# Keeping the parts of k for the second group of rows, and the order of the first weight chunk's work

## The chip, the cores and the metric

One core of one Trainium2 chip. The metric is the time of one execution on the device, in microseconds (us), as the median of several runs. Every time below comes from the profile or from the runs of the kernel before.

## What is computed

Attention that keeps the 32 largest scores of a row, then a dense layer pair with a leaky activation, then a layer that sends each row to one of eight experts. Inputs are float32. q, k and v are 4 x 8 x 576 x 64 (batch, heads, rows, head width).

```python
scores = scale * np.matmul(q, k.transpose(0, 1, 3, 2))
kth = np.partition(scores, -top_k, axis=-1)[..., -top_k:-top_k + 1]
scores = np.where(scores >= kth, scores, -1000000000.0)
attn = softmax(scores)
x = np.matmul(attn, v)                      # 2304 rows of 512
h = x @ w_in                                # 512 x 2048
x = (np.maximum(h, 0.0) + alpha * np.minimum(h, 0.0)) @ w_out
# then: rows with x @ w_skip > 0 add gate * relu(x @ w1[e]) @ w2[e], e by argmax(x @ w_gate)
```

## The kernel before

**Units of work.** A batch has 576 rows: four blocks of 128 (units 0 to 3) and a rest of 64. Heads go in pairs, so a batch has four pairs, and unit 4 takes the rest of both heads of a pair together (the mixed unit). A batch is done in two groups of rows, units 0 and 1, then units 2, 3 and 4; within a group all four pairs follow each other. So each pair of a batch comes up twice, once in either group: 32 pair visits, 80 steps of one unit. After a group its rows go through the dense layers (`moe1`, lines 611 and 657), as a list of small pieces that is dealt out over the following steps.

**Order.** Nothing is scheduled by the machine: `main` writes the instructions out step by step. A step has 14 slots, and the table `STEP` says which part of which unit is issued in which slot. Unit kx+2 has its scores made on PE (`scores`, L417, L411), unit kx+1 has its selection rounds on DVE (`round`, L447, L450) after the fold (`fold`, L438), unit kx its exponentials on ACT (L472) and weights on DVE (`weights`, L480), unit kx-1 is transposed on PE (`turn`, L510 to L516) and copied by ACT (`evac`; R is line 528), unit kx-2 is multiplied by v on PE (`values`, L539, L543) and put into x (`out`, L550, L552). Each engine runs its list in order.

**Heads.** Before a pair's first unit comes its head, `heads`: `load` brings q and k (L321, and L323 for the rest rows), `turn(0)` transposes q on PE, `turn_t` the rest rows of q and k, `turn(1)` k. TensorE multiplies in a short float32 format (F32R), so each operand is kept as two parts: `part` (L330, L331) lets ACT write the high part and a float32 copy `raw_` (two buffers), and POOL subtracts (`sub`, L108) to get the low part. The scores are the sum of three products of parts. The k parts of a pair are a tile `kT` of 2 x 640 columns a partition, in two buffers; L353 copies the rest columns to its other end. `qbd` is the mixed unit's q (L358, L361). The head's pieces are spread over the steps of the pair before it: `hq` is shared out so that each step gets an equal number, the first of them in slot 4, the next in slot 5. Both visits of a pair do the whole head, with the q of their own rows and the whole of k.

**Weights of the dense layers.** They come as 32 chunks of 512 KB in a packed format, and `convert` turns each into parts: ACT copies three times (L277, L279, L281), DVE joins bits (`bits`, L285) and then issues the load of the chunk `AHEAD` = 3 further on, POOL splits (`split`, L291 and L108), SP stores the result (`store`, L297, L300). This goes on during batch 0. The raw chunks lie in halves of the three `wr` buffers, which later hold the dense layers' weights.

**POOL and DVE.** `sub` lets POOL's subtraction wait for DVE's last fold instruction issued before it (`gate`), and `between` holds back `g` parts of the dense layers from slot 9 to slot 1 of the next step. A `ra` tile (six buffers) lives from ACT's line 621 to POOL's `g` part; `held` counts those and lets a new piece begin only below six.

Of the kernel before, what the change touches and what calls it, by code (L numbers as in the profile page):

```python
# [34 lines left out]
AHEAD = 3  # L35
# [12 lines left out]
CV = 4  # L48
# [10 lines left out]
def kernel(  # L59
# [176 lines left out]
    raws, converted, pads = {}, set(), {}  # L236
# [30 lines left out]
    def convert(i):  # L267
# [37 lines left out]
        return none * (CV - 1 if i != 1 else 3 * CV) + [bits] + none * (CV - 1) + [split] + none * CV + [store]  # L305


    def heads(b, p, i, us):
# [3 lines left out]
        own = ((full[0], full[-1] + 1), (0, SF))  # L312
        nats = {}

        def load():
            tail = att.tile([128, 2, D], F32, name="nat_t", tag="nat_t", bufs=2)
            for s, src in enumerate((q, k)):
                nat = att.tile([128, SF, 2, D], F32, name="nat", tag="nat", bufs=2)
                r0, r1 = own[s]
                for h in range(2):  # L320
                    (nc.scalar if s and quick[0] else nc.sync).dma_start(nat[:, r0:r1, h, :],  # L321
                                      src[b, 2 * p + h, 0:SB, :].rearrange("(p r) d -> p r d", p=128)[:, r0:r1])
                (nc.scalar if s and quick[0] else nc.sync).dma_start(tail[s * TL:(s + 1) * TL], src[b, 2 * p:2 * p + 2, SB:S, :].rearrange("h t d -> t h d"))  # L323
                nats[s] = nat
            nats[2] = tail
# [8 lines left out]
        def turn(s):  # L334
            if s == 0:

                hd["q"] = att.tile([128, 2, SB], F32R, name="qT", tag="qT", bufs=2)
                hd["k"] = att.tile([128, 2, S + TL], F32R, name="kT", tag="kT", bufs=2)
# [6 lines left out]
            late.append((HL, lambda: part(hd["k"][:, :, TL:TL + SB] if s else hd["q"][:, :, c0:c1], pt)))  # L345

        def turn_t():
# [3 lines left out]
            def copies():  # L351
                part(hd["k"][:, :, 0:TL], pt[:, TL:128])
                nc.gpsimd.tensor_copy(hd["k"][:, :, S:S + TL], hd["k"][:, :, 0:TL].bitcast(F32))  # L353
# [22 lines left out]
        return hd, [lambda: turn(0), turn_t, lambda: turn(1)]  # L376
# [12 lines left out]
    class Unit:  # L389
# [10 lines left out]
        def scores(self):  # L400
# [4 lines left out]
            for j in range(2):  # L405
                for h in range(self.nh):
                    self.ps[h, j] = ptile() if h and j else psS.tile([128, 512], F32, name="ps", tag="ps")
                for i, (a, b_) in enumerate(((0, 0), (1, 0), (0, 1))):
# [5 lines left out]
                    for h in range(2):  # L414
                        gp = slice(h * 64, (h + 1) * 64)
                        c0 = TL * (1 - h) + j * HALF
                        nc.tensor.matmul(self.ps[h, j][:, 0:HALF], lhsT=hd["q"][gp, a, u * 128:(u + 1) * 128],  # L417
# [162 lines left out]
    def moe1(xx, cols, x2t, base):  # L580
# [20 lines left out]
        def up(wi, f, sg, half, first):  # L601
# [16 lines left out]
            ra = moe.tile([128, 320], F32, name="ra", tag="ra", bufs=6)[:, 0:n]  # L618
# [56 lines left out]
        for hf in range(nhf):  # L675
            for f in range(hf * fs, (hf + 1) * fs):
                for sg, (c0, c1) in enumerate(cols):
                    for half in range(2):
                        one = f % 2 == 0 and sg == 0 and half == 0
                        if half == 0:  # L680
                            parts.append((lambda: room() and held[0] < 6, None))
# [423 lines left out]
    def main(work, exact, hooks=(lambda: [], lambda: [])):  # L1105
# [113 lines left out]
        if not exact:  # L1219
# [3 lines left out]
            for i in range(AHEAD):  # L1223
# [15 lines left out]
        hq.clear()  # L1239
        if exact:  # L1240
# [243 lines left out]
```

## Time and profile before

| | |
|---|---|
| median of 3 runs | 1085.13 us (1083.98 to 1085.79) |
| profiled execution, its own time | 1084.56 us |
| its span in the profile | 1082.8 us |
| busy: PE, DVE, ACT, POOL | 935.1, 922.2, 703.0, 429.7 us |
| mean granted clock of TensorE | 0.947 |
| DMA | 254.13 MB, 235 GB/s in the mean |

Batch 0 runs from the start to about 215 us, the others take some 196 us each, attention ends at about 815 us, the last group's dense layers at about 905 us, and the experts follow.

How to read the rows: times are us from the span's start. A row of a timeline gives start, duration, engine, line, operation, out<-in, shapes and count, and in brackets the engine's idle time before it and what ended it. Merged instructions of a pipelined engine can overlap, so their count times one duration is more than what they take. A row of busy times gives the stretch, its length, the busy us of PE, PEld (weight loads), DVE, ACT and POOL with their instructions, TensorE's granted clock as a share of 2.4 GHz, the DMA engines' busy share and GB/s. A row of the chain gives start, length and what the end of the program waited for then. Engines with a q are their queues.

### The profile page before, as it was taken

What the parts mean: (1) busy time and instruction counts of PE and PEld (TensorE: products, weight loads), DVE (VectorE), ACT (ScalarE), POOL (GpSimd) and SP (SyncE); (2) the same over time, 40 slices, a digit from 0 to 9 for tenths busy, and PEclk for the clock granted to TensorE, in tenths of its full rate; (3) what the DMA queues carried; (4) which work ended last, traced back from release to release, by engine and by line L of the source; (5) the groups of instructions that cost most, each with busy time, mean ns of one, the idle gap of its engine ahead of it and who ended that gap; (6) DMA issues with size and microseconds to landing.
All of it is one profiled execution on the core that took longest, in us unless ns stands there. A gap on an engine that the chain in (4) does not pass through costs nothing.

```text
span 1082.8 us, 21930 instructions
## 1 busy us (share of the span) xinstructions
PE 935.1 (86%) x7270; PEld 844.8 (78%) x7270; DVE 922.2 (85%) x2943; ACT 703.0 (65%) x1804; POOL 429.7 (40%) x577
## 2 busy tenths in 40 slices
PE   4435668998999989989998998999899998798995
PEld 2224458898998878989998898999789897587884
DVE  4999999999999799999989998999895233899972
ACT  6969857765865576567657766866674343597871
POOL 5766754422542334344224433532341330427221
PEclk9966669998999999999999999999999999899998
DMA  7888985665656566766656666665556798899960
GB/s 218 296 276 214 304 259 184 223 214 172 223 190 229 164 214 195 256 222 225 213 167 215 213 252 224 205 225 195 174 203 235 271 349 340 279 356 397 346 234 15
DMA packets 154282, 254.13 MB, mean 235 GB/s; under 512 B 78062, under 2 KB 110830, under 8 KB 137776
## 3 DMA queue, kind: packets, MB, share of 16 engines
q1 hardware_dynamic: 150464, 247.84, 67.6%
q0 software_dynamic: 2496, 4.50, 1.2%
q8 instruction: 59, 0.97, 0.4%
q14 instruction: 63, 0.52, 0.1%
q10 hardware_dynamic: 1200, 0.30, 0.1%
HBM read 224.20 MB, written 29.71 MB: 234 GB/s over the span
## 4 chain that ended last, share of the span: by engine, by line
PE 41%; DVE 37%; issue 6%; ACT 6%; POOL 5%; DMA 5%; SPq 0%; POOLq 0%; DVEq 0%; ACTq 0%
PE pm L657 14%; DVE v L447 8%; PE pm L611 6%; DVE F L438 5%; DVE Ex L480 5%; DVE m L438 4%; DVE F L450 4%; PE px L1033 4%; PE pm L1015 4%; PE px L543 4%; DVE ra L624 3%; PE ps L417 2%; PE pt L510 2%; POOL cv L108 2%; PE pm L723 1%
## 5 line engine op out<-in xcount | busy, mean ns | idle before, releaser
L611 PE MATMUL pm<-x,wr 128*128 128x256 f32 (+1 forms) x1536 | 248.8, 309 | 17.0 <-DVE ra L624 10.3
L657 PE MATMUL pm<-g,wr 128*128 128x256 f32 (+1 forms) x1536 | 236.0, 304 | 4.1 <-DMA wr<-wout 3.5
L611 PEld LDWEIGHTS pm<-x,wr 128*128 128x128 f32 x1536 | 215.7, 194 | 28.2 <-DVE ra L624 14.8
L657 PEld LDWEIGHTS pm<-g,wr 128*128 128x128 f32 x1536 | 210.2, 190 | 9.9 <-issue 4.1
L447 DVE MAX8 v<-F 128x8 f32<-128x72 f32 (+2 forms) x576 | 212.9, 405 | 0.8
L108 POOL TENSOR_TENSOR g<-ra,g 128x256 fp32r<-128x256 f32 (+1 forms) x128 | 104.9, 824 | 185.8 <-ACT g L630 95.6
L480 DVE SCALAR_TENSOR_TENSOR Ex<-sb,v,Ex 128x577 f32<-128x577 f32 x144 | 129.8, 928 | 0.0
L450 DVE MATCH_REPLACE8 F<-v,F 128x72 f32<-128x72 f32 (+1 forms) x432 | 122.8, 289 | 0.0
L422 ACT ACTIVATE sb<-ps 128x288 f32<-128x288 f32 x224 | 80.0, 411 | 62.2 <-PE ps L417 51.3
L630 ACT ACTIVATE g<-ra 128x256 fp32r<-128x256 f32 (+1 forms) x128 | 57.1, 446 | 75.1 <-DVE ra L624 73.3
L472 ACT ACTIVATE Ex<-sb,st 128x576 f32<-128x576 f32 x144 | 104.7, 775 | 0.1
L522 ACT ACTIVATE PT<-pt 128x512 f32<-128x512 f32 x144 | 86.9, 604 | 16.3 <-PE pt L510 15.6
L624 DVE SCALAR_TENSOR_TENSOR ra<-ra,slope,pm 128x256 f32<-128x256 f32 (+1 forms) x128 | 64.6, 505 | 32.1 <-ACT ra L621 30.2
L543 PE MATMUL px<-PT,vt 128*64 128x128 f32 (+1 forms) x1280 | 89.2, 286 | 0.0
L510 PE MATMUL pt<-ident,Ex 128*128 128x128 f32 x576 | 85.9, 281 | 2.6 <-ACT sb L422 2.6
L108 POOL TENSOR_TENSOR x<-xf,x 128x128 fp32r<-128x128 f32 (+1 forms) x80 | 49.3, 617 | 96.0 <-ACT x L552 94.8
L417 PE MATMUL ps<-kT,qT 64*128 64x288 f32 x576 | 79.5, 348 | 6.1 <-ACT kT L330 2.0
L543 PEld LDWEIGHTS px<-PT,vt 128*64 128x64 f32 x1280 | 70.1, 147 | 9.9 <-issue 1.8
L417 PEld LDWEIGHTS ps<-kT,qT 64*128 64x128 f32 x576 | 61.4, 210 | 19.3 <-issue 9.4
L510 PEld LDWEIGHTS pt<-ident,Ex 128*128 128x128 f32 x576 | 70.7, 146 | 3.9 <-ACT sb L422 3.5
L621 ACT ACTIVATE ra<-pm 128x256 f32<-128x256 f32 (+1 forms) x128 | 52.4, 409 | 30.9 <-PE pm L611 28.7
L438 DVE TENSOR_TENSOR F<-m 128x144 f32<-128x144 f32 (+2 forms) x240 | 70.2, 344 | 0.0
(431 smaller groups left out, 1834.8 us busy)
## 6 DMA issues: line engine op xcount, KB each, us to landing
wr<-win SPq DMA_DIRECT2D x64, 1024.0 KB, 4.9
wr<-wout SPq DMA_DIRECT2D x64, 1024.0 KB, 4.9
wraw<-in_moe_w_dram SPq DMA_DIRECT2D x88, 512.0 KB, 6.3
wr<-in_moe_w_in_dram SPq DMA_DIRECT2D x16, 512.0 KB, 6.1
vt<-in_v_dram SPq DMA_DIRECT2D x32, 256.0 KB, 2.8
win<-cv SPq DMA_DIRECT2D x16, 512.0 KB, 4.8
wr<-in_moe_w_out_dram SPq DMA_DIRECT2D x16, 512.0 KB, 5.6
wout<-cv SPq DMA_DIRECT2D x32, 256.0 KB, 4.1
```

What stands on the lines that cost most here:

```text
L108: i = nc.gpsimd.tensor_tensor(o, a, b, op=OP.subtract)
L417: nc.tensor.matmul(self.ps[h, j][:, 0:HALF], lhsT=hd["q"][gp, a, u * 128:(u + 1) * 128], rhs=hd["k"][gp, b_, c0:c0 + HALF], **se)
L438: gate[0] = nc.vector.tensor_tensor(o[:, n_], a[:, n_, 0:w], a[:, n_, w:2 * w], op=op)
L447: nc.vector.max(v8[:, h, r, :], F[:, h, 0:w])
L450: nc.vector.match_replace(out=F[:, h, 0:w], in_to_replace=v8[:, h, r, :], in_values=F[:, h, 0:w], imm_value=NEG)
L472: nc.scalar.activation(self.Ex[:, h, :], self.sb[:, h, :], AF.Exp, bias=self.st[:, 0, h:h + 1], scale=0.125)
L480: nc.vector.scalar_tensor_tensor(self.Exp[:, cs], self.sbp[:, cs], v8[:, h, 3, 7:8], self.Exp[:, cs], op0=OP.is_ge, op1=OP.mult, accum_out ...
L510: nc.tensor.transpose(pt[:, c * 128:(c + 1) * 128], P[:, c0:c0 + 128], ident)
L543: nc.tensor.matmul(x[h * 64:(h + 1) * 64, 0:n], lhsT=hd["vt"][:, h, c, :], rhs=rhs, start=False, stop=(c == SF - 1))
L611: nc.tensor.matmul(hp[:, 0:n], lhsT=w[:, (f % 2) * 8 + a * 4 + d, :], rhs=x[:, d, c0:c1], start=(i == 0), stop=(i == 3 * KD - 1))
L624: nc.vector.scalar_tensor_tensor(ra, ra, slope[:, f:f + 1], hp[:, 0:n], op0=OP.mult, op1=OP.add)
L657: nc.tensor.matmul(op_[:, 0:n], lhsT=w[:, 2 * f + a, :], rhs=g[(hf + ch) * 8 + f, sg][:, gg, 0:n], start=(i == 0), stop=(i == ni - 1))
```

## The change

Each pair's k parts are kept in a place of their own (`kT0` to `kT3`, one buffer each) from a pair's first visit of a batch to its second. The second visit loads no k but the rest rows (which share a transpose with q's), does not transpose k, and makes no k parts. The q tile has room for 256 columns instead of 512, and `ra` five buffers instead of six, with the limit in `moe1` lowered alike. `AHEAD` is 4: three chunks are loaded first, the fourth after the first heads' loads, and from then on `bits` loads four ahead. Chunk 0's `bits` and `split` are issued one slot after its copies.

```diff
-AHEAD = 3
+AHEAD = 4
...
-        return none * (CV - 1 if i != 1 else 3 * CV) + [bits] + none * (CV - 1) + [split] + none * CV + [store]
+        if i == 0:
+            return none + [bits, split] + none * (2 * CV) + [store]
+        return none * (CV - 1 if i > 1 else 3 * CV) + [bits] + none * (CV - 1) + [split] + none * CV + [store]
...
+        fresh = us[0] == 0
...
             for s, src in enumerate((q, k)):
+                if s and not fresh:
+                    nc.sync.dma_start(tail[TL:2 * TL], src[b, 2 * p:2 * p + 2, SB:S, :].rearrange("h t d -> t h d"))
+                    continue
...
-                hd["q"] = att.tile([128, 2, SB], F32R, name="qT", tag="qT", bufs=2)
-                hd["k"] = att.tile([128, 2, S + TL], F32R, name="kT", tag="kT", bufs=2)
+                hd["q"], hd["c0"] = att.tile([128, 2, 256], F32R, name="qT", tag="qT", bufs=2), own[0][0] * 128
+                if fresh:
+                    kept[p] = att.tile([128, 2, S + TL], F32R, name="kT", tag=f"kT{p}", bufs=1)
+                hd["k"] = kept[p]
...
-                part(hd["k"][:, :, 0:TL], pt[:, TL:128])
-                nc.gpsimd.tensor_copy(hd["k"][:, :, S:S + TL], hd["k"][:, :, 0:TL].bitcast(F32))
+                if fresh:
+                    part(hd["k"][:, :, 0:TL], pt[:, TL:128])
+                    nc.gpsimd.tensor_copy(hd["k"][:, :, S:S + TL], hd["k"][:, :, 0:TL].bitcast(F32))
...
-        return hd, [lambda: turn(0), turn_t, lambda: turn(1)]
+        return hd, [lambda: turn(0), turn_t] + ([lambda: turn(1)] if fresh else [])
...
-            ra = moe.tile([128, 320], F32, name="ra", tag="ra", bufs=6)[:, 0:n]
+            ra = moe.tile([128, 320], F32, name="ra", tag="ra", bufs=5)[:, 0:n]
...
-                            parts.append((lambda: room() and held[0] < 6, None))
+                            parts.append((lambda: room() and held[0] < 5, None))
...
-            for i in range(AHEAD):
+            for i in range(AHEAD - 1):
                 conv_load(*convs[i])
...
+        if not exact:
+            conv_load(*convs[AHEAD - 1])
```

The order of SP's queue at the head of the program, before (the `wr` rows are the loads of chunks 3, 4, and 5 and 6; `win` is the store of chunk 0; `nat` are q and k of the third pair, `vt` and `vbd` v of the second):

```order
L369 DMA vt<-in_v_dram 128x2x256
L372 DMA vbd_93<-in_v_dram 64x64 x2
L258 DMA wr<-in_moe_w_in_dram 128x4x256
L297 DMA win_123<-cv 128x1024
L258 DMA wr<-in_moe_w_in_dram 128x4x256
L321 DMA nat<-in_q_dram 128x2x64 x2
L323 DMA nat_t<-in_q_dram 64x2x64
L321 DMA nat<-in_k_dram 128x4x64 x2
L323 DMA nat_t<-in_k_dram 64x2x64
L258 DMA wr<-in_moe_w_in_dram 128x4x256 x2
```

and after the change (the `wr` rows are chunks 3, 4 and 5):

```order
L258 DMA wr<-in_moe_w_in_dram 128x4x256
L379 DMA vt<-in_v_dram 128x2x256
L382 DMA vbd_93<-in_v_dram 64x64 x2
L258 DMA wr<-in_moe_w_in_dram 128x4x256
L297 DMA win_123<-cv 128x1024
L258 DMA wr<-in_moe_w_in_dram 128x4x256
L328 DMA nat<-in_q_dram 128x2x64 x2
L330 DMA nat_t<-in_q_dram 64x2x64
L328 DMA nat<-in_k_dram 128x4x64 x2
L330 DMA nat_t<-in_k_dram 64x2x64
```

The load of chunk 3 moved ahead of the second pair's v, that of chunk 4 ahead of the store of chunk 0, and that of chunk 5 ahead of the third pair's q and k.

The order on ACT in the second group of batch 2, two steps in which the head of the third pair is made (PT and R are the unit's transposes, `ps` the head's), before:

```order
L330 ACTIVATE qT<-ps 128x256
L331 ACTIVATE raw__7629<-ps 128x256
L330 ACTIVATE kT<-ps 128x64
L331 ACTIVATE raw__7640<-ps 128x64
L358 ACTIVATE raw__7645<-ps 128x64
L361 ACTIVATE qbd_95<-ps 64x64 x2
L522 ACTIVATE PT<-pt 128x512
L552 ACTIVATE x<-xf 128x128
L522 ACTIVATE PT<-pt 128x512
L455 ACTIVATE st<-v_7279 128x1
L527 ACTIVATE PT<-px 128x128
L528 ACTIVATE R<-px 128x128
```

and after the change:

```order
L337 ACTIVATE qT<-ps 128x256
L338 ACTIVATE raw__7443<-ps 128x256
L532 ACTIVATE PT<-pt 128x512
L562 ACTIVATE x<-xf 128x128
L532 ACTIVATE PT<-pt 128x512
L465 ACTIVATE st<-v_7100 128x1
L537 ACTIVATE PT<-px 128x128
L538 ACTIVATE R<-px 128x128
```

The copies of k's rest columns and of k are gone; the mixed unit's q (L358 and L361, now L368 and L371) moved to the next step, five rows further on.

The order on PE in the same second step, before and then with the change:

```order
L657 MATMUL pm<-g,wr 128x320 x6
L343 MATMUL ps<-ident,nat 128x128 x4
L510 MATMUL pt<-ident,Ex_143 128x128 x4
L657 MATMUL pm<-g,wr 128x320 x6
L510 MATMUL pt<-ident,Ex_143 128x128 x4
```

```order
L667 MATMUL pm<-g,wr 128x320 x6
L358 MATMUL ps<-ident,nat_t 128x128
L520 MATMUL pt<-ident,Ex_143 128x128 x4
L667 MATMUL pm<-g,wr 128x320 x6
L520 MATMUL pt<-ident,Ex_143 128x128 x4
```

The four transposes of k are gone, and the transpose of the rest rows stands there, which was in the step before.

## Rows read from the trace of the kernel before

**Rows 1.** the page, part 4: the chain of waits by engine

```profile
PE 41%; DVE 37%; issue 6%; ACT 6%; POOL 5%; DMA 5%; SPq 0%; POOLq 0%; DVEq 0%; ACTq 0%
```

**Rows 2.** busy time by stage, second groups of batches 1 and 3

```profile
300.00:413.00 113.00, 103.80 (x905) 95.48 (x900) 103.76 (x382) 71.24 (x215) 42.59 (x65) 0.98 0.60 198
...
697.00:812.00 115.00, 108.24 (x945) 100.36 (x944) 109.78 (x409) 76.73 (x227) 41.61 (x66) 0.99 0.60 201
```

**Rows 3.** the same by stretch, head of the program

```profile
10.00:20.00 10.00, 4.74 (x23) 3.15 (x23) 7.94 (x29) 8.54 (x20) 4.21 (x6) 1.00 0.70 187
20.00:30.00 10.00, 1.33 (x8) 0.98 (x8) 5.86 (x16) 5.38 (x10) 7.24 (x8) 1.00 0.96 283
...
140.00:160.00 20.00, 12.51 (x75) 10.23 (x75) 19.01 (x60) 10.70 (x32) 13.35 (x16) 0.61 0.95 291
```

**Rows 4.** timeline of DVE, head; in brackets the wait before it

```profile
18.23 0.69 DVE L285 SCALAR_TENSOR_TENSOR cv<-cv 128x512 int32<-128x512 int32 x1 [1.31 <-ACT cv L281]
...
24.38 0.91 DVE L285 SCALAR_TENSOR_TENSOR cv<-cv 128x512 int32<-128x512 int32 x1 [2.67 <-ACT cv L281]
...
29.60 1.13 DVE L285 SCALAR_TENSOR_TENSOR cv<-cv 128x512 int32<-128x512 int32 x1 [0.71 <-ACT cv L281]
...
36.24 0.69 DVE L285 SCALAR_TENSOR_TENSOR cv<-cv 128x512 int32<-128x512 int32 x1 [0.90 <-ACT cv L281]
```

**Rows 5.** timeline of ACT, head

```profile
22.38 0.67 ACT L277 ACTIVATE cv<-wr 128x512 f32<-128x512 f32 x1 [1.36 <-DMA wr<-in_moe_w_in_dram]
...
27.60 0.67 ACT L277 ACTIVATE cv<-wr 128x512 f32<-128x512 f32 x1 [3.25 <-DMA wr<-in_moe_w_in_dram]
```

**Rows 6.** timeline of SP's queue, head; last row: of PE

```profile
17.14 0.35 SPq L297 DMA_DIRECT2D win<-cv  x1
...
22.27 1.15 SPq L258 DMA_DIRECT2D wr<-in_moe_w_in_dram  x2
...
31.20 0.69 PE L343 MATMUL ps<-ident,nat 128*128 128x128 f32 x2 [9.33 <-ACT sb L422]
```

**Rows 7.** lines 343 and 330: ns least/median/most, first and last start

```profile
L343 PE MATMUL ps<-ident,nat x192: 270/272/477, 3.9 to 789.7; 128*128 128x128 f32 x192
...
L330 ACT ACTIVATE kT<-ps x64: 203/426/628, 5.7 to 790.0; 128x512 fp32r<-128x512 f32 x32, 128x64 fp32r<-128x64 f32 x32
```

**Rows 8.** timeline of ACT, then PE, third pairs of batches 1 and 2

```profile
347.68 0.22 ACT L358 ACTIVATE raw__4531<-ps 128x64 f32<-128x64 f32 x1 [1.11 <-POOL qT L108]
...
350.04 0.49 PE L539 MATMUL px<-PT,vbd 128*128 128x128 f32 x2 [1.75 <-ACT R L528]
...
550.36 0.49 PE L539 MATMUL px<-PT,vbd 128*128 128x128 f32 x2 [0.99 <-ACT R L528]
```

**Rows 9.** chain of waits in batch 1, then the timeline of DVE

```profile
354.50 0.44 PE ps L343 x4
...
365.05 0.18 DVE L767 TENSOR_REDUCE rc<-lg 128x3 f32<-128x24 f32 x1 [3.80 <-ACT lg L732]
```

**Rows 10.** timeline of DVE, then POOL, in batch 2

```profile
527.79 0.80 DVE L480 SCALAR_TENSOR_TENSOR Ex<-sb,v,Ex 128x577 f32<-128x577 f32 x1
...
528.52 1.84 DVE L480 SCALAR_TENSOR_TENSOR Ex<-sb,v,Ex 128x577 f32<-128x577 f32 x1
...
555.94 1.84 DVE L438 TENSOR_TENSOR F<-sb 128x576 f32<-128x576 f32 x1
...
528.25 1.49 POOL L108 TENSOR_TENSOR kT<-raw__7365,kT 128x512 fp32r<-128x512 f32 x1 [4.62 <-ACT raw__7365 L331]
```

**Rows 11.** timeline of POOL, then DVE, in batch 0

```profile
153.09 0.83 POOL L108 TENSOR_TENSOR kT<-raw__1561,kT 128x64 fp32r<-128x64 f32 x1
153.98 0.70 POOL L353 CAST kT<-kT 128x128 fp32r<-128x128 f32 x1
...
164.01 0.48 DVE L624 SCALAR_TENSOR_TENSOR ra<-ra,slope,pm 128x256 f32<-128x256 f32 x1 [2.73 <-ACT ra L621]
```

**Rows 12.** busy time and granted clock of one stretch

```profile
250.00:270.00 20.00, 16.95 (x129) 15.73 (x128) 18.24 (x84) 11.03 (x30) 5.19 (x9) 0.74 0.48 144
```

More of the change, by code (lines that the diff above doesn't have):

```diff
@@ L235 @@
     wout32 = w_out.bitcast(I32)
-    raws, converted, pads = {}, set(), {}
+    raws, converted, pads, kept = {}, set(), {}, {}
     todo, late, convq, rowq = [], [], [], []
@@ L312, in heads @@
         own = ((full[0], full[-1] + 1), (0, SF))
+        fresh = us[0] == 0
+        assert own[0][1] - own[0][0] <= 2
         nats = {}
@@ L344, in turn @@
                                     ident)
-            late.append((HL, lambda: part(hd["k"][:, :, TL:TL + SB] if s else hd["q"][:, :, c0:c1], pt)))
+            late.append((HL, lambda: part(hd["k"][:, :, TL:TL + SB] if s else hd["q"][:, :, 0:c1 - c0], pt)))
         def turn_t():
@@ L416, in scores @@
                         c0 = TL * (1 - h) + j * HALF
-                        nc.tensor.matmul(self.ps[h, j][:, 0:HALF], lhsT=hd["q"][gp, a, u * 128:(u + 1) * 128],
+                        nc.tensor.matmul(self.ps[h, j][:, 0:HALF], lhsT=hd["q"][gp, a, u * 128 - hd["c0"]:(u + 1) * 128 - hd["c0"]],
                                          rhs=hd["k"][gp, b_, c0:c0 + HALF], **se)
```

## Prediction

> **What bounds the kernel now.** I read the page's chain of waits first: PE has 41% of the time that decides the end and DVE 37% [rows 1], so neither engine is the bound by itself. The busy time by stage says why. In the second group of rows of batch 1 (300 to 413 us) PE is busy 103.80 and DVE 103.76 of 113 us; in that of batch 3 (697 to 812 us) 108.24 and 109.78 of 115 [rows 2]. Both are nearly full, each waits for the other now and then, and work that only one of them loses is lost to the end only where the chain runs over that engine. ACT (71 to 77 us there) and POOL (about 42) have room, but they stand between the two: what they do late, PE or DVE waits for.
>
> The head of the program is another matter. From 10 to 30 us DVE is busy 7.94 and 5.86 of 10 us [rows 3]. Its waits there end with ACT's last copy of a weight chunk (L281), and ACT itself waits 1.36 and 3.25 us for the load of the chunk [rows 4, 5]. Further on in batch 0 DVE has hardly a wait left: from 140 to 160 us it is busy 19.01 of 20 [rows 3].
>
> **The change, part by part.** It does what it says: the order of the built program has no second-group k work, and without the rows of the heads the order on PE, DVE, ACT and POOL is that of before, apart from the first chunk's split on POOL. So the limit of five `ra` tiles moves no instruction; I cost it at nothing, and the cover is that POOL's `g` parts end several us before the tile is wanted again (ACT shows no wait for a `g` part).
>
> *Head.* In the kernel before, the load of chunk 4 stands behind the store of chunk 0, which waits for POOL's split until 17.14 us, and the load of chunk 5 stands behind the q and k loads of the third pair, at 22.27 us [rows 6]. Now the split of chunk 0 stands ahead of the second pair's parts on POOL, the load of chunk 4 goes ahead of the store, and that of chunk 5 ahead of the q and k loads. Both should have landed when ACT asks. Of DVE's three waits (2.67, 0.71 and 0.90, 4.28 together [rows 4]) one piece stays: ACT is free for chunk 4 from 21.02 us (22.38 less its wait), so DVE still waits some 1.3 us for it. Gain **3.0 us**, an estimate. Its ends are 0 and 4.3: zero if the DMA engines, 0.96 busy from 20 to 30 us and 0.95 from 140 to 160 [rows 3], only pass the same bytes in another order. I take a value near the upper end since they are 0.70 busy from 10 to 20 us [rows 3], which is where the loads move to. What the loads are moved past: the store of chunk 0 (nobody reads it for 100 us) and the loads of the third pair, which land later by about two chunk loads; PE takes those only at 31.20 us, after 9.33 us of waiting for something else [rows 6]. The early split puts two POOL instructions under DVE's first fold; that can stretch the fold by about 1.1 us, as below, and DVE's wait of 1.31 us at 18.23 [rows 4] hides it; without that cover the gain would be 1.9.
>
> *PE, 16 pairs.* Each second-group pair loses four transposes of k. One takes 0.27 us in the rows, but they overlap: four have 0.44 us of the chain [rows 7, 9]. 16 x 0.44 = 7.0 us of PE in all, of which only four pairs have them on the chain, one in batch 3, one in batch 2, two in batch 1.
>
> *ACT, 16 pairs.* Two copies of 512 columns and two of 64 go: 0.2 to 0.6 us each [rows 7], some 1.6 us a pair, beside other work. What counts is a wait. A pair's small part (`turn_t`) needs a third buffer `raw_` while there are two, so ACT waits for POOL's q part: 1.11 us at 347.68, and PE behind it 1.75 us for R; in batch 2 PE's wait is 0.99, in batch 3 the same pattern returns [rows 8]. With no k part in between, q and the mixed unit's q have two buffers, and the latter moves to the next step. Those PE waits should go.
>
> *POOL, 16 pairs.* One subtraction of 512 columns, one of 64 and one copy go. Where POOL works on SBUF while DVE runs an instruction with two inputs, both are stretched. DVE's weights instruction takes 0.80 us alone and 1.84 under the k part, its fold 1.84 under the next one, and POOL's part takes 1.49 [rows 10]. Six of the twelve k parts of the later batches fall on such instructions, two in each batch; the rest fall on MAX8 and MATCH_REPLACE, which are not stretched. The Trainium skill, SBUF — State Buffer, section "SBUF: two separate sides", says the shared ports are an exclusive lock, the loser blocking for the other's whole instruction. The rows agree only in the sum: DVE goes on, 1.04 us late, and POOL is late as well. By the rule with POOL's 1.49 a collision would cost 1.49 instead of 1.04, and the two that I count below would give 0.9 us more.
>
> *DMA.* 32 loads of k of 128 KB go from SP's queue; they were asked for a pair ahead of their transposes, and I cost them at nothing, up and down.
>
> *What of it lies on the path.* Batch 0: POOL's small k part and its copy (0.83 and 0.70 us at 153 us) stand ahead of the x part that PE waits for, and DVE waits 2.73 us at 164.01 at the end of that chain [rows 11]. Gain **1.5**, ends 0 and 2.7. Batch 1: here PE leads up to the logits, where DVE waits 3.80 us [rows 9], so PE's 1.75 and 0.44 count: **2.2**. Batches 2 and 3: the first collision (1.04) lies in a stretch that DVE leads, then PE's wait (0.99) and four transposes (0.44) where PE leads: **2.5** each. Against it: the x part, which POOL does behind the k part, now starts earlier and falls on the same DVE instruction; I take off 0.3 us for each of the two collisions counted, **0.6**. What is late next is the x part itself and, in batch 1, DVE.
>
> **Sum**: 3.0 + 1.5 + 2.2 + 2.5 + 2.5 - 0.6 = 11.1 us. The profiled execution took 1084.56 us (span 1082.8), 0.57 below the median of the runs, 1085.13. 1084.56 - 11.1 = 1073.5, and that is the forecast: **1073.5 us**. Lower bound of the gain: only the two DVE collisions less their give-back, 1.5, so 1083.1. Upper bound: 4.3 + 2.7 + 7.2, and the four collisions that I left out at 1.04 each: 18.4, so 1066.2.
>
> **The rivals.** (a) *Hidden*: the DMA engines hold the first 160 us (0.95 busy at its end [rows 3]) and the other engine takes every gap in the later batches. For it: both engines are within 5% to 8% of full [rows 2]. Against it: DVE itself gets shorter by the collisions. Gain 0 to 2: about 1083.5 us. Chance 0.08. (b) *Slower, by TensorE's clock.* PE loses work and waits more for DVE in the second groups. Already from 250 to 270 us, with PE busy 16.95 of 20, the granted clock is 0.74 [rows 12]: 0.26 of the way down, so half of those 20 us ran at 1.2 GHz instead of 2.4, and PE lost 5.2 us of work. If three more such places arise in stretches that PE leads, 15.6 us are lost against 11.1 won: 1089 us; from the third on it decides. Against it: the stretches of batches 1 and 3 are at 0.98 and 0.99 [rows 2] although PE waits there, and the change also takes away PE waits. The Trainium skill, TensorE: Matmul & The Clock Gate, section "Part 1: The HAM clock gate", says that the lower clock is the default and activity lifts it, which speaks against a change that takes work from PE. Chance 0.05. (c) *Gains add up*: DVE gets shorter where it leads and PE where it leads, so that the four other collisions and PE's remaining R waits count, and the later stages of the chain fall into better places: 1064 us. For it: gaps of both kinds stand close together. Chance 0.07.
>
> **How the numbers follow.** The forecast's case has 0.80. Its bounds 1066.2 and 1083.1 together with a third of (c) give the range: **1065.0 to 1082.5**, which leaves out (b), most of (a) and the far side of (c). A measurement of this kernel tells a change from none from about 0.2% (2.2 us) on. Faster: 0.80 + 0.07, and a little of (a): 0.88. Within 0.2%: the rest of (a): 0.07. Slower: 0.05.
>
> **What would show it.** In the profile after: DVE's waits at L285 between 20 and 40 us down to about 1.3 us, ACT's waits for chunk loads there gone, and DVE's eighth chunk (at 36.24 us before) about 3 us earlier; no 1.84 us weights instruction on DVE beside a k part; PE's waits for R in the second groups under 0.5 us; attention ending some 11 us earlier and the tail, from 812 us on, of the same length. The forecast is wrong if the attention's end moves by under 3 us, if the clock in the second groups falls under 0.95, or if the tail grows by what the attention lost.

## The result and the profile after

The changed kernel takes **1066.37 us** in the median (1066.3 to 1066.6, 4 runs) against 1085.46 of the kernel before: ratio 0.9822, 95% interval 0.9803 to 0.9841, so 19.1 us faster. The forecast was 1073.5 in a range from 1065.0 to 1082.5. Sign and range hold; the gain is some 8 us larger than forecast. The profiled execution took 1066.43 us, its span 1064.6.

DVE runs the same instructions in the same order in both kernels. So the start of one DVE instruction in both traces tells how much has been won by then:

| DVE instruction near | before | after | earlier by | forecast up to there |
|---|---|---|---|---|
| the end of the head | 52.8 | 51.0 | 1.75 | 3.0 |
| second group of batch 0, its middle | 152.5 | 149.2 | 3.25 | |
| end of batch 0 | 219.8 | 210.7 | 9.11 | 4.5 |
| start of batch 1's second group | 296.4 | 286.4 | 10.02 | |
| end of batch 1 | 415.0 | 399.4 | 15.60 | 6.7 |
| end of batch 2 | 615.2 | 596.9 | 18.29 | 8.9 |
| end of batch 3 | 811.7 | 791.7 | 20.00 | 11.1 |
| end of the span | 1082.8 | 1064.6 | 18.2 | 11.1 |

The surplus came in two places: from 152 to 220 us, and in the second group of batch 1. Batches 2 and 3 gave 2.7 and 1.7 us where 2.2 each was forecast, and the tail gave 1.8 us back. A share of one batch is uncertain by some 2 us: the changed kernel once more against the run with five `ra` tiles (both below, on two other chips) has 5.9, 6.5, 4.4 and 2.1 us in batches 0 to 3.

The page's chain of waits by engine, which was DVE's nearly as much as PE's [rows 1], is now PE's:

```profile
PE 53%; DVE 28%; ACT 4%; DMA 3%; issue 3%; POOL 2%; SPq 0%; POOLq 0%; ACTq 0%; DVEq 0%
```

Busy time by stage, the same pieces of work as in [rows 2] (columns as there: PE, PEld, DVE, ACT, POOL, then clock, DMA share, GB/s), and the stretch of batch 0 that [rows 3] ends with:

```profile
289.50:397.40 107.90, 100.62 (x891) 92.62 (x886) 101.31 (x381) 66.89 (x201) 33.71 (x55) 1.00 0.60 200
678.50:792.00 113.50, 107.51 (x931) 99.80 (x930) 107.22 (x409) 72.21 (x213) 32.07 (x56) 0.97 0.58 197
...
140.00:160.00 20.00, 16.44 (x132) 14.50 (x132) 19.69 (x62) 12.51 (x38) 10.76 (x14) 0.85 0.90 297
```

The second group of batch 1 lost 3.2 us of PE's busy time, 2.5 of DVE's and 9 of POOL's, and is 5.1 us shorter: more than either engine lost, so waits went too. From 140 to 160 us the granted clock is 0.85 where it was 0.61; the changed kernel on another chip has 0.69 there.

**Head.** Timeline of DVE, line 285 (two chunks of those in [rows 4], then the eighth), the early split's neighbour (line 448, which was 438), and ACT's only wait of 0.4 us or more for a chunk between 20 and 38 us:

```profile
11.47 1.80 DVE L448 TENSOR_TENSOR m<-sb 128x576 f32<-128x576 f32 x1 [0.85 <-ACT sb L432]
...
23.87 1.00 DVE L285 SCALAR_TENSOR_TENSOR cv<-cv 128x512 int32<-128x512 int32 x1 [1.23 <-ACT cv L281]
29.48 1.36 DVE L285 SCALAR_TENSOR_TENSOR cv<-cv 128x512 int32<-128x512 int32 x1
35.16 1.74 DVE L285 SCALAR_TENSOR_TENSOR cv<-cv 128x512 int32<-128x512 int32 x1
...
34.98 0.67 ACT L277 ACTIVATE cv<-wr 128x512 f32<-128x512 f32 x1 [0.40 <-DMA wr<-in_moe_w_in_dram]
```

The waits went as forecast (1.23 left of 2.67, the others gone), but part of them came back as longer instructions beside POOL: the first fold took 0.76 us before and takes 1.80. The eighth chunk is 1.1 us earlier, not 3.

**Batch 0.** Before, ACT stood still behind POOL. Timelines of ACT and PE of the kernel before:

```profile
153.16 0.22 ACT L358 ACTIVATE raw__1566<-ps 128x64 f32<-128x64 f32 x1 [3.19 <-POOL qT L108]
...
154.25 0.30 ACT L552 ACTIVATE x<-xf 128x128 fp32r<-128x128 f32 x1
...
154.60 1.23 PE L611 MATMUL pm<-x,wr 128*128 128x256 f32 x4 [2.09 <-ACT x L552]
```

The same places after (ACT, then POOL, then DVE):

```profile
147.36 0.31 ACT L562 ACTIVATE x<-xf 128x128 fp32r<-128x128 f32 x1 [0.97 <-DVE xf L560]
...
148.62 0.97 POOL L108 TENSOR_TENSOR x<-xf,x 128x128 fp32r<-128x128 f32 x1
...
156.25 0.48 DVE L634 SCALAR_TENSOR_TENSOR ra<-ra,slope,pm 128x256 f32<-128x256 f32 x1
```

ACT no longer waits for POOL, x goes out as soon as DVE has it, and DVE's wait of 2.73 us [rows 11] is down to 0.13. Two shorter waits of DVE for `ra` beside it are gone as well; before:

```profile
158.54 0.48 DVE L624 SCALAR_TENSOR_TENSOR ra<-ra,slope,pm 128x256 f32<-128x256 f32 x1 [0.82 <-ACT ra L621]
...
185.58 0.48 DVE L624 SCALAR_TENSOR_TENSOR ra<-ra,slope,pm 128x256 f32<-128x256 f32 x1 [0.90 <-POOL qbd L108]
```

At these three instructions together DVE's lead over the kernel before grows by 4.5 us.

**Waits for R.** Busy time by line, PE's first multiply of the values (line 539 before, 549 after; x count, then busy us, mean ns, and the idle time before it with what ended it), 140 us to the end of attention, before:

```profile
L539 PE MATMUL px<-PT,vbd 128*128 128x128 f32 (+1 forms) x136 | 27.4, 284 | 8.2 <-ACT R L528 8.2
```

and after:

```profile
L549 PE MATMUL px<-PT,vbd 128*128 128x128 f32 (+1 forms) x137 | 26.6, 276 | 0.2 <-ACT R L538 0.2
```

Nearly all the waits for R are gone, 8.2 us of PE's idle time before; the forecast had counted 3.7 of them (1.75 and twice 0.99).

**Collisions.** DVE in batch 2, the two instructions that took 1.84 us each [rows 10]:

```profile
512.22 0.81 DVE L490 SCALAR_TENSOR_TENSOR Ex<-sb,v,Ex 128x577 f32<-128x577 f32 x1
...
539.49 0.75 DVE L448 TENSOR_TENSOR F<-sb 128x576 f32<-128x576 f32 x1
```

DVE's lead over the kernel before grows by 1.03 us at the first and by 1.10 at the second, which the forecast had left out. In between, DVE loses 0.80 us of it where it then waits longer for PE (2.06 us instead of 1.25).

**Batch 1.** The logits and two `ra` tiles behind them. DVE before, beside the wait of 3.80 us at the logits [rows 9], and then after:

```profile
375.83 0.48 DVE L624 SCALAR_TENSOR_TENSOR ra<-ra,slope,pm 128x256 f32<-128x256 f32 x1 [1.27 <-ACT ra L621]
...
380.99 0.48 DVE L624 SCALAR_TENSOR_TENSOR ra<-ra,slope,pm 128x256 f32<-128x256 f32 x1 [1.16 <-ACT ra L621]
```

```profile
351.41 0.18 DVE L777 TENSOR_REDUCE rc<-lg 128x3 f32<-128x24 f32 x1 [2.52 <-ACT lg L742]
...
361.11 0.48 DVE L634 SCALAR_TENSOR_TENSOR ra<-ra,slope,pm 128x256 f32<-128x256 f32 x1 [0.19 <-issue]
...
365.42 0.47 DVE L634 SCALAR_TENSOR_TENSOR ra<-ra,slope,pm 128x256 f32<-128x256 f32 x1
```

DVE's lead grows by 1.28 us at the logits and by 2.3 at the two `ra` tiles. Two collisions, which the forecast did not count in this batch, give 1.02 and 1.10, of which 0.86 is lost again in a wait for PE.

**Tail.** Timeline of PE, the last block of multiplies, before and then after:

```profile
1066.56 5.72 PE L1033 MATMUL px<-x,hs 128*128 128x512 f32 x24 [2.32 <-DVE orow L1041]
```

```profile
1047.02 7.29 PE L1043 MATMUL px<-x,hs 128*128 128x512 f32 x24 [2.32 <-DVE orow L1051]
```

The same 24 multiplies take 1.57 us longer: nothing in them was changed, they now lie in a stretch of lower granted clock (0.77 from 1047 to 1054.4 us, against 1.00 from 1066 to 1072.5 before). That is most of the 1.8 us given back. In the fourteen traces of this case the block takes 7.15 to 7.33 us nine times and 5.7 five times. The last experiment below, which keeps the whole change, is among the five, so the change does not force the longer block.

### The profile page after: what moved, and what is told of

Same layout as the page of the kernel before. It is cut to its first block, busy times and chain, and to the rows that moved or that the text cites. A ratio compares the mean times of both kernels' runs of the same rounds, so it can differ in the third digit from the quotient of the medians.

```text
span 1064.6 us, 21663 instructions
## 1 busy us (share of the span) xinstructions
PE 925.9 (87%) x7206; PEld 834.4 (78%) x7206; DVE 915.7 (86%) x2943; ACT 684.1 (64%) x1740; POOL 386.0 (36%) x529
## 4 chain that ended last, share of the span: by engine, by line
PE 53%; DVE 28%; ACT 4%; DMA 3%; issue 3%; POOL 2%; SPq 0%; POOLq 0%; ACTq 0%; DVEq 0%
PE pm L667 18%; PE pm L621 10%; DVE v L457 6%; PE px L553 5%; DVE Ex L490 4%; PE px L1043 4%; PE pm L1025 4%; DVE F L448 3%; DVE F L460 3%; PE ps L427 3%; PE pt L520 3%; DVE ra L634 3%; DVE m L448 3%; DMA wr<-wout 2%; PE pm L733 1%
## 5 line engine op out<-in xcount | busy, mean ns | idle before, releaser
L621 PE MATMUL pm<-x,wr 128*128 128x256 f32 (+1 forms) x1536 | 244.8, 307 | 15.4 <-DVE ra L634 10.6
L621 PEld LDWEIGHTS pm<-x,wr 128*128 128x128 f32 x1536 | 212.9, 191 | 27.1 <-DVE ra L634 15.9
L108 POOL TENSOR_TENSOR x<-xf,x 128x128 fp32r<-128x128 f32 (+1 forms) x80 | 46.3, 579 | 112.2 <-ACT x L562 111.2
L448 DVE TENSOR_TENSOR F<-m 128x144 f32<-128x144 f32 (+2 forms) x240 | 66.6, 329 | 0.0
```

Of the source, the lines that this page charges most:

```text
L108: i = nc.gpsimd.tensor_tensor(o, a, b, op=OP.subtract)
L448: gate[0] = nc.vector.tensor_tensor(o[:, n_], a[:, n_, 0:w], a[:, n_, w:2 * w], op=op)
L621: nc.tensor.matmul(hp[:, 0:n], lhsT=w[:, (f % 2) * 8 + a * 4 + d, :], rhs=x[:, d, c0:c1], start=(i == 0), stop=(i == 3 * KD - 1))
```

## The experiments

The twelve runs were made in three sittings of four, each on a chip of its own, on which the kernel before takes a little longer (medians 1090.14, 1089.57 and 1088.39 us). So ratios to the kernel before of the same sitting are compared. The first sitting has the two halves of the change, the smaller `ra` ring and the run without POOL's parts; the second has the changed kernel again, PE's transposes, the old step and the third buffer; the third has the rest. Where a trace of before is needed, the run with five `ra` tiles, from the chip of the first sitting, stands in for it.

**Which half of the change?** The change without its head:

```diff
-AHEAD = 4
+AHEAD = 3
...
-        if i == 0:
-            return none + [bits, split] + none * (2 * CV) + [store]
...
-            for i in range(AHEAD - 1):
+            for i in range(AHEAD):
...
-            conv_load(*convs[AHEAD - 1])
```

> The change without its head: k is kept in four places, but three chunks are loaded ahead as before, chunk 0 is split and stored as before. Theory 1 (the head gives what DVE's first waits show, 1.75 us by 52 us of the span, and all the rest comes from the k work that is gone): 1068 us, 16 to 18 us faster than before, and at the end of batch 0 DVE is 6 to 7 us earlier than before. Rival 2 (the head also carries the gain inside batch 0, where DVE is 9.1 us earlier at 215 us, because its chunks are through sooner): about 1075 us, and DVE at the end of batch 0 at most 3 us earlier than before. Rival 3 (head and k add less alone than together): 1070 to 1073 us.

Measured: 1070.96 us, ratio 0.9818 (0.9803 to 0.9833). The k part alone gives 18 to 21 us. In its trace DVE is 5.2 us earlier than before at 204 us, after being 1.4 late at 52 (6.4 earlier and 0.4 late against the stand-in). Rival 2 falls, and Rival 3 with it: by the ratio, k alone gives rather more than the 16 to 18 us of Theory 1, not less.

The same edit the other way round, on the kernel before, is the head alone:

> The kernel before with the head of the change alone: four chunks ahead, chunk 0's bits and split at once, the fourth load behind the first heads. Theory 1: 1.5 to 2.5 us faster than before, about 1083.3 us, with the k parts' collisions and waits all still there. Rival 2: about 1076 us. My forecast had 3.0 for it, so 1082.4 us. If the early split stretches DVE's first folds and nothing is won by it, 1085.

Measured: 1087.6 us, ratio 0.9974 (0.9963 to 0.9985): 1.6 to 4.0 us. The trace has DVE 2.65 us earlier than before at 52 us and no more than that at 204 us (3.6 and 3.4 against the stand-in, from the same chip). The forecast's 3.0 stands for the head by itself.

The smaller ring of `ra` tiles, on the kernel before:

```diff
-            ra = moe.tile([128, 320], F32, name="ra", tag="ra", bufs=6)[:, 0:n]
+            ra = moe.tile([128, 320], F32, name="ra", tag="ra", bufs=5)[:, 0:n]
...
-                            parts.append((lambda: room() and held[0] < 6, None))
+                            parts.append((lambda: room() and held[0] < 5, None))
```

> The kernel before with five ra tiles in place of six, and the limit that goes with them. All theories that I hold: no change, 1085 us, within 0.2%. If the sixth tile was worth something, slower by 1 us or more, and then the change had to win that back too.

Measured: 1088.59 us, ratio 0.9989 (0.9977 to 1.0001). No cost.

Last, the changed kernel itself, on the chip of the second sitting:

> The changed kernel unaltered, beside the next three on one chip. Expected: ratio to before 0.982, as in the result. Theory 3 (head and k do not add: k alone gave 0.9818): nothing left for the head to add, so 0.980 to 0.983; if they add, 0.9795 or less, since the head alone gave 0.9974.

Measured: 1068.25 us, ratio 0.9805 (0.9789 to 0.9821). Together with 0.9822 of the first chip and 0.9818 for k alone, the head's share within the whole change is between nothing and some 3 us: whether the two parts add stays open.

**Which engine's share of the k work?** The work was put back into the changed kernel step by step. First everything but POOL's:

```diff
-                if s and not fresh:
-                    nc.sync.dma_start(tail[TL:2 * TL], src[b, 2 * p:2 * p + 2, SB:S, :].rearrange("h t d -> t h d"))
-                    continue
...
+        def idle(pt):
+            n = pt.shape[1]
+            raw = att.tile([128, 512], F32, name="raw_", tag="raw_", bufs=2)[:, 0:n]
+            nc.scalar.activation(raw, pt, AF.Copy)
+            nc.scalar.activation(raw, pt, AF.Copy)
...
+            if s and not fresh:
+                late.append((HL, lambda: idle(pt)))
+                return
...
+                else:
+                    idle(pt[:, TL:128])
...
-        return hd, [lambda: turn(0), turn_t] + ([lambda: turn(1)] if fresh else [])
+        return hd, [lambda: turn(0), turn_t, lambda: turn(1)]
```

> The changed kernel with the second groups' k loads, transposes and ACT copies put back (both copies go to the staging tile, nobody reads it), without POOL's subtractions and copy. Against the changed kernel it prices PE's and ACT's part, against the head alone it prices POOL's part. Theory 1a (POOL's parts, by stretching DVE's two-input instructions and by standing ahead of the x part, carry the gain): 1067 to 1070 us. Rival 1b (PE's four transposes and the waits of PE for ACT carry it): 1076 to 1080 us. By my forecast's terms (16 pairs, PE's transposes 0.44 on four of them and waits for R of 1.75 and 0.99, these already gone without POOL's part): 1068.2 us.

Measured: 1080.78 us, ratio 0.9920 (0.9904 to 0.9936); its own runs spread from 1076.1 to 1083.9. Theory 1a falls: with the head and without POOL's parts, 8.7 of the 21 us are left. The rest is not all work of PE and ACT, though. With three pieces in the head again, `turn_t` is back in its old step, which the expectation overlooked, and the runs below price that by itself at 4.8 us.

The same without ACT's copies (loads and PE's transposes stay):

```diff
-                late.append((HL, lambda: idle(pt)))
                 return
...
-                else:
-                    idle(pt[:, TL:128])
```

> The changed kernel with the second groups' k loads and the k transposes on PE put back (four of a pair, nobody reads them), without ACT's copies and without POOL's parts. It splits what the run without POOL's parts (0.992 of before) left between PE and ACT. Theory 4 (ACT's k copies, 1.6 us a pair, stand ahead of the copies of ra, R and the logits that PE and DVE wait for): as the changed kernel within 3 us, 0.982 to 0.985. Rival 5 (the four transposes are what counts, 16 times 0.44 us and more where they sit ahead of the dense layers): 0.988 to 0.991.

Measured: 1077.12 us, ratio 0.9888 (0.9873 to 0.9903). So rival 5's figure came out. But this kernel, too, has `turn_t` back in its old step. Two runs take that apart. The old step alone, with an empty third piece:

```diff
-        return hd, [lambda: turn(0), turn_t] + ([lambda: turn(1)] if fresh else [])
+        return hd, [lambda: turn(0), turn_t] + [(lambda: turn(1)) if fresh else (lambda: None)]
```

> The changed kernel with the second groups' small transposes (turn_t) issued in the step where they stood before, one step earlier than the change has them; nothing else. If the move counts (the mixed unit's q copies sharing a step with the q copies again): slower than the changed kernel by 1 to 3 us, PE's waits for R back. If k's work alone was the load: as the changed kernel within 1 us.

Measured: 1073.18 us, ratio 0.9849 (0.9833 to 0.9864). Without any k work the mere place of one transpose, three small copies and two small subtractions is worth 4.8 us. PE's waits for R came back only in part (1.5 us in its trace, 0.2 in the changed kernel's), and ACT's waits for POOL's q part not at all, so the staging buffer is not the reason.

The old step and the k loads (the `continue` above taken out, no transposes):

> The changed kernel with the second groups' k loads put back and the small transposes in the old step; no transposes, copies or subtractions of k. Between the run with the old step alone (0.985) and the one with loads and PE's transposes (0.989) it tells the DMA's part from PE's. Forecast's step (loads cost nothing): 0.984 to 0.986, as the old step alone. Rival (32 loads of 128 KB crowd SP's queue or the DMA engines): 0.988 or more.

Measured: 1073.53 us, ratio 0.9862 (0.9848 to 0.9876), inside the interval of the run before: the best estimate for the loads is 1.4 us, which is within the error of nothing.

Read downwards, each difference is one share (in thousandths, times 1.089 us; each is uncertain by about 2 us, and the rows come from three chips):

| kernel | ratio | what goes to the next row | us |
|---|---|---|---|
| before | 1 | the head | 2.8 |
| head alone | 0.9974 | POOL's k parts | 5.9 |
| without POOL's parts | 0.9920 | ACT's k copies and their hold on the staging buffers | 3.5 |
| loads and PE's transposes | 0.9888 | PE's k transposes | 2.8 |
| old step and loads | 0.9862 | the k loads | 1.4 |
| old step | 0.9849 | `turn_t` one step later | 4.8 |
| changed kernel | 0.9805 | | 21.2 in all |

**The staging buffer.** The forecast had put the waits for R on the third `raw_` that a head wants. This is the kernel before with one more:

```diff
-            raw = att.tile([128, 512], F32, name="raw_", tag="raw_", bufs=2)[:, 0:pt.shape[1]]
+            raw = att.tile([128, 512], F32, name="raw_", tag="raw_", bufs=3)[:, 0:pt.shape[1]]
...
-                raw = att.tile([128, 512], F32, name="raw_", tag="raw_", bufs=2)[:, 0:TL]
+                raw = att.tile([128, 512], F32, name="raw_", tag="raw_", bufs=3)[:, 0:TL]
```

> The kernel before with three staging buffers raw_ in place of two, and nothing else. My forecast put PE's waits for R (1.75 us in batch 1, 0.99 in batches 2 and 3) on ACT's wait of 1.11 us for the third of these buffers. If that is the mechanism: 2 to 4 us faster, ratio 0.996 to 0.998. Theory 4 (ACT's k copies themselves make R late, the buffer hardly matters): 0.9995 to 1.0005.

Measured: 1081.63 us, ratio 0.9932 (0.9919 to 0.9945): **7.4 us**, about twice what was expected. The mechanism is shown, and its size was wrong: ACT's twelve waits for POOL's q part are gone, and PE's waits for R in the attention come to 3.3 us in its trace against 8.8 in the stand-in's (8.2 on the first chip). Timeline of PE, then DVE, in batch 1 and the busy time of three stretches (the clock is the third column from the end), of the stand-in for before, which is from another chip:

```profile
349.81 0.49 PE L539 MATMUL px<-PT,vbd 128*128 128x128 f32 x2 [1.76 <-ACT R L528]
...
366.33 0.18 DVE L767 TENSOR_REDUCE rc<-lg 128x3 f32<-128x24 f32 x1 [6.57 <-ACT lg L732]
...
348.00:352.00 4.00, 2.24 (x23) 1.74 (x24) 4.00 (x23) 2.40 (x8) 1.82 (x6) 0.86 0.23 94
352.00:356.00 4.00, 4.00 (x28) 3.71 (x27) 3.99 (x9) 1.62 (x5) 0.00 (x0) 0.71 0.00 0
...
372.00:376.00 4.00, 4.00 (x38) 3.61 (x38) 3.67 (x19) 1.92 (x3) 2.87 (x5) 0.65 0.67 195
```

and of the kernel with three buffers:

```profile
347.43 0.49 PE L539 MATMUL px<-PT,vbd 128*128 128x128 f32 x2 [0.49 <-ACT R L528]
...
362.43 0.18 DVE L767 TENSOR_REDUCE rc<-lg 128x3 f32<-128x24 f32 x1 [2.51 <-ACT lg L732]
...
348.00:352.00 4.00, 4.00 (x43) 3.66 (x42) 4.00 (x20) 1.55 (x6) 0.79 (x4) 1.00 0.01 2
352.00:356.00 4.00, 4.00 (x32) 3.99 (x31) 4.00 (x6) 3.64 (x10) 2.27 (x2) 1.00 0.75 250
...
368.00:372.00 4.00, 3.95 (x47) 3.68 (x48) 3.77 (x19) 2.62 (x5) 2.76 (x5) 1.00 0.78 217
```

PE waits 1.76 us for R with PE busy 2.24 of 4 us, and the granted clock falls: 0.86 and 0.71 of full in the two stretches are 0.14 and 0.29 of 4 us of work, at most 1.7 us, lost on top of the wait. DVE's wait for the logits is then 6.57 us; with the third buffer it is 2.51 and the clock stays at 1.00. The wait and the fall together thus cost about 4 us at the logits. This pair alone does not take them apart, since both went. But the kernel before on the first chip has the same wait and keeps its clock there (last section), and its DVE waits 3.80 us at the logits [rows 9]. By that, some 1.3 us are the wait and 2.8 the fall, as far as traces from three chips can be compared.

The same aim without a buffer, on the kernel before: the small transposes after k's.

```diff
+        if us[0]:
+            return hd, [lambda: turn(0), lambda: turn(1), turn_t]
         return hd, [lambda: turn(0), turn_t, lambda: turn(1)]
```

> The kernel before with the order of a second-group pair's three transposing steps changed: q, then k, then the small one, so that the small one (turn_t) stands in the next step, near where the changed kernel has it; all of k's work still done, two staging buffers as before. Theory 6 (the wait for the third staging buffer is what both the third buffer and the move take away): the gain of the third buffer (0.9932 of before), so 0.992 to 0.995, ACT's waits for POOL's q part at the small copy gone. Rival 7 (the move gains by spreading ACT's and PE's work, 4.9 us even where no buffer waits): less than 0.991. If k's transposes, now earlier, collide anew: 0.997 or more.

Measured: 1085.45 us, ratio 0.9970 (0.9958 to 0.9982): 3.3 us, less than either theory, and in the third range of the expectation. The waits for the staging buffer are gone, but the k parts, now a step earlier, fall on other instructions: of the twelve k parts of 512 columns in the second groups of batches 1 to 3, eleven now run beside a weights or fold instruction of DVE, where six did. DVE, then POOL, in batch 2 of this kernel:

```profile
517.04 1.71 DVE L482 SCALAR_TENSOR_TENSOR Ex<-sb,v,Ex 128x577 f32<-128x577 f32 x1
...
527.37 1.06 DVE L482 SCALAR_TENSOR_TENSOR Ex<-sb,v,Ex 128x577 f32<-128x577 f32 x1
...
516.85 1.28 POOL L108 TENSOR_TENSOR kT<-raw__7224,kT 128x512 fp32r<-128x512 f32 x1 [0.99 <-ACT raw__7224 L331]
```

The first takes 0.80 us where no k part stands beside it. The second is the one that took 1.84 before [rows 10]. So waits were traded for collisions. This speaks for the collision as a cost in itself: 0.91 us here, 1.04 in the forecast.

**Trying to go further.** Chunk 0's split put back to its old place in the changed kernel:

```diff
-        if i == 0:
-            return none + [bits, split] + none * (2 * CV) + [store]
-        return none * (CV - 1 if i > 1 else 3 * CV) + [bits] + none * (CV - 1) + [split] + none * CV + [store]
+        return none * (CV - 1 if i != 1 else 3 * CV) + [bits] + none * (CV - 1) + [split] + none * CV + [store]
```

> The changed kernel with chunk 0's bits, split and store back where they stood before; four chunks ahead and the later fourth load stay. The early split runs beside DVE's first fold, which the profile shows stretched from 0.76 to 1.80 us. If that price is paid in full: 1 us faster than the changed kernel, 0.9795. If the early split is what brings the head's gain: 1 to 3 us slower, 0.982 to 0.983. My forecast held it free of cost, hidden by DVE's wait of 1.31 us: same or slower.

Measured: 1067.56 us, ratio 0.9811 (0.9796 to 0.9827): as the changed kernel. That the wait covers the stretched fold, as forecast, fits this, but a price of 1 us would not show within the error.

And `turn_t` one step later still, behind the next pair's load:

```diff
-                hq.append(ahead[i + 1][0]["load"])
+                hq.insert(len(hq) - (len(parts) == 2), ahead[i + 1][0]["load"])
```

> The changed kernel with the second groups' small transposes one step later still, and the load of the next pair one step earlier in their place. Theory 7 (spreading goes on to pay): 1 to 3 us faster than the changed kernel, 0.978 to 0.9795. Theory 6 (there is no staging wait left in the changed kernel, so nothing to gain): within 1 us, 0.980 to 0.982; the earlier load may stretch waits by contention, at most 1 us.

Measured: 1067.03 us, ratio 0.9802 (0.9789 to 0.9814): as the changed kernel. Nothing more is won by spreading within the error; no version tried beats the changed kernel beyond it.

## Why the prediction was right in sign and range, and short by 8 us

The range held narrowly: 1066.37 lies 0.2 us inside the 1066.2 that the forecast had for all of its gains at their upper ends. That the sign and the range hold is no proof of the sum, of which several terms were too small.

- **Head, 3.0 us: right.** The trace has 1.75, the head alone 2.8 (1.6 to 4.0). Loads and ACT's waits went as said; the sign that DVE's eighth chunk would be 3 us earlier was wrong (1.1), since the chunk instructions themselves got longer beside POOL.
- **Batch 0, 1.5 us: mis-sized, measured 7.4** (9.11 less 1.75). The failed step is "POOL's small k part and its copy stand ahead of the x part that PE waits for". It went on from POOL's two rows and did not look at ACT, which waited 3.19 us for the third staging buffer there, ahead of the copy of x that PE waits for. The whole wait at 164.01 went, and the two others for `ra`, 4.5 us together, where 1.5 stood in the sum. k alone gives most of the batch (6.6 us between 52 and 204 us in the run without the head). The buffer is only a part of it: with a third buffer alone DVE gains 2.0 us on the stand-in between 152 and 220 us, where the change gains 5.9. The clock from 140 to 160 us, 0.61 before [rows 3] and 0.85 or 0.69 after, goes the same way; how much it adds stays open.
- **Batch 1, 2.2 us: mis-sized, measured 6.5.** The step "a pair's small part needs a third buffer" had the mechanism right, and the third buffer alone shows it at 7.4 us for the whole kernel where the forecast's R waits came to 3.7. ACT waited for POOL's q part 12 times, 9.84 us in all, not only at the places of [rows 8]. But the place was wrong: at the logits, where the forecast had its 2.2, only 1.28 came. The rest came at the `ra` tiles behind them and at the two collisions that the forecast had left out of this batch. On the first chip, where this was measured, the clock did not fall at the wait for R. It fell once behind the logits (0.72 and 0.86 from 368 to 376 us) and not after the change, which may have a part in the waits for `ra`.
- **Batches 2 and 3, 2.2 each: measured 2.7 and 1.7, in part by luck.** A second collision in each batch, 1.1 us of DVE's lead, was not in the sum, and neither were the 0.8 us in each that DVE lost again in a wait for PE.
- **"Only four pairs have the transposes on the chain": not refuted.** Three of the four, 1.3 of 7.0 us, stand in the sum, since batch 1 has only one of its two; measured 2.8, uncertain by 2.
- **Collisions: right in price, too few counted, and misread.** They cost 1.04 each, and DVE's lead grew at those that were left out as well. POOL's share is 5.9 us; the forecast's terms for it were 2.1 less 0.6, and batch 0's 1.5. The Trainium skill, SBUF — State Buffer, section "SBUF: two separate sides", has the loser block for the other's whole instruction. The trace agrees, where the forecast said that DVE goes on: in [rows 10] the weights instruction ends 0.62 us after POOL's part (530.36 and 529.74), and so does the one at 517.04 above (518.75 and 518.13). In the kernel before, 46 of the 47 weights instructions of 577 columns that begin inside one of POOL's subtractions, 0.2 us or more before its end, end 0.61 or 0.62 us after it. So what a collision costs DVE is what is left of POOL's part when DVE's instruction begins, less 0.18 us (1.22 and 1.04 in [rows 10], 1.09 and 0.91 at 517.04), and not POOL's whole 1.49, as the forecast worked it out. POOL is held up in the same way: its k part takes about 1.28 us beside MAX8 and 1.45 to 1.78 where it begins inside a two-input instruction of DVE, and in all seven such cases of that kernel it ends 1.13 to 1.16 us after that instruction.
- **The move of `turn_t`: no term of its own.** The forecast named it in half a sentence as a reason why the R waits go. It is worth 4.8 us. In the traces of the two kernels on one chip, 3.5 us apart in span, the old step has one more fall of the clock in batch 1; the changed kernel, then the old step:

```profile
352.00:356.00 4.00, 4.00 (x31) 3.92 (x31) 2.18 (x11) 0.93 (x4) 0.00 (x0) 0.73 0.09 37
356.00:360.00 4.00, 2.98 (x19) 2.00 (x18) 3.72 (x24) 3.16 (x13) 0.51 (x2) 0.84 0.45 168
360.00:364.00 4.00, 4.00 (x50) 3.70 (x49) 3.33 (x17) 2.10 (x5) 3.27 (x5) 1.00 0.82 225
364.00:368.00 4.00, 2.99 (x24) 2.55 (x23) 3.36 (x9) 3.81 (x14) 3.18 (x5) 1.00 0.67 123
```

```profile
352.00:356.00 4.00, 4.00 (x34) 3.96 (x34) 1.10 (x9) 0.24 (x2) 0.00 (x0) 0.82 0.39 160
356.00:360.00 4.00, 3.31 (x18) 2.53 (x17) 3.79 (x19) 2.43 (x8) 0.60 (x2) 0.76 0.15 55
360.00:364.00 4.00, 3.61 (x30) 3.14 (x32) 3.71 (x21) 2.80 (x8) 2.00 (x3) 0.67 0.87 271
364.00:368.00 4.00, 3.95 (x34) 3.58 (x33) 1.77 (x9) 2.11 (x8) 2.22 (x4) 0.90 0.55 89
```

  The missing clock of the four rows, times 4 us, is 1.7 us of work in the first and 3.4 in the second. The changed kernel itself has no such fall there on the first chip, so one trace of each does not tell what belongs to the move. How much of the 4.8 us is this stays open.
- **`ra` ring and loads at nothing: right** within the error (0.9989; 0.0013 between the two runs).
- **Tail of the same length: wrong by 1.8 us**, most of it by the clock in the last block.
- **Rivals.** (c), gains add up, 1064 us, is nearest to what happened. (b), the clock, did not come: the Trainium skill, TensorE: Matmul & The Clock Gate, section "Part 1: The HAM clock gate", has activity lift the clock, and the forecast's rival feared for PE's lost work. No such loss shows here: the mean clock is 0.947 before and 0.948 after. Nor does taking waits away show in the mean: the third buffer, which takes no work away, has 0.946 to 0.954 in its runs, and the kernel before beside it 0.940 to 0.955.

## What to carry to other kernels

Where two engines are both nearly full, don't price removed work by the few places at which the chain of one execution happens to run over it: here DVE's lead grew at the collisions that were left out as well. List every wait of a helper engine for a staging buffer, in all batches; twelve waits of ACT, 9.84 us, were worth 7.4 us and could have been had for one buffer. And when a change drops a piece from a list that is dealt out over steps, price the move of the pieces behind it by itself: here it was worth as much as the transposes and the loads together.

## What the hardware showed beyond that

The same wait of PE does not always cost the clock. On the first chip the kernel before has the wait of 1.75 us at 350.04 [rows 8] and keeps its clock in the stretches around it:

```profile
348.00:352.00 4.00, 2.25 (x28) 1.69 (x29) 4.00 (x22) 2.60 (x9) 1.98 (x7) 1.00 0.17 72
352.00:356.00 4.00, 4.00 (x37) 3.83 (x34) 4.00 (x10) 2.53 (x8) 0.00 (x0) 1.00 0.13 20
```

With nearly the same busy time (2.25 against 2.24 of 4 us) the stand-in on another chip fell to 0.86 and 0.71. The head alone, on that same chip, has the wait too (1.75 us at 346.38) and fell to 0.93 and 0.64. But the fall does not need this wait: the changed kernel, which does not have it, fell to 0.73 and 0.84 from 352 us on in its second trace and kept 1.00 from 328 to 392 us in its first. The stand-in's DVE falls 2.6 us behind the first chip's trace between 355 and 384 us and another 2.2 by 583 us; its span is 4.9 us longer in all (1087.7 against 1082.8). So a good part of its longer time sits at such places. What a change that touches PE's waits is worth can therefore differ by some us from one execution to another; with one trace of a kernel on each chip, the chip can't be told from the execution.
